# Sparse attention followed by an ELU layer pair: first loads in halves, four output tiles, and a new order of work

## The chip, the core and the metric

The kernel runs on one core of a Trainium2 chip. The core has five engines that run side by side, each with its own queue that it works off in order: TensorE (PE, matrix products into PSUM), VectorE (DVE), ScalarE (ACT, functions such as exp and ln, and copies), GpSimd (POOL, which here issues loads) and SyncE (SP, which here issues stores and DMA transposes). Transfers run on 16 DMA engines. The metric is the time of the device for one execution, in microseconds (us).

## The reference

Eight batches, eight heads, 576 positions, 64 features. Heads 0 to 3 see the last 32 positions (local), heads 4 to 7 every 32nd position back (strided). The result is laid out as 4608 tokens of 512 features and goes through two layers with an ELU between them.

```python
scores = scale * np.matmul(q, k.transpose(0, 1, 3, 2))
mask_local = (rel >= 0) & (rel < stride)
mask_strided = (rel >= 0) & (pos[None, :] % stride == pos[:, None] % stride)
scores = np.where(masks[None, :, :, :], scores, -1000000000.0)
attn = np.exp(scores - max); attn = attn / (sum(attn) + 1e-09)
x = np.matmul(attn, v)             # to (4608, 512)
h = x @ w_in                       # (512, 2048)
g = np.where(h > 0.0, h, np.exp(np.minimum(h, 0.0)) - 1.0)
out = g @ w_out                    # (2048, 512)
```

## The kernel before

**Tiles.** Tokens of a batch are held in eight interleaved sequences (`NS`), so that local and strided windows become small dense blocks. A *pair* is two heads of one kind of one batch: key `2s1` is batch 2, strided, pair 1; `l` is local. Each pair is worked in two halves, u = 0 and 1. q and k are transposed so that features lie on partitions (`qT`, `kT`); for batches 0 to 2 PE does this with an identity matrix and a copy out of PSUM, from batch 3 on a DMA transpose does it. The attention result goes to `xT`, features on partitions, all tokens. The layers run in nine *chunks* of 512 tokens: sixteen tiles m of the hidden layer, then four tiles kk of 128 output tokens.

**Order.** The order of all work is written out by hand in the string `ORDER` (lines 35 to 149), which a loop at the end (line 680) turns into calls. Since every engine works in the order in which its instructions were issued, this string is the queue of each engine. The letters: `w` warm-up matmuls on zeros; `F` masks; `K` cast of a staged head to bf16 (line 379; q on DVE, k on ACT); `T` transposes on PE (392, 395); `c`/`C` their copy out of PSUM on DVE/ACT (403 to 407); `S` scores (431); `e` exponential (438, ACT); `m` mask (445, 451, DVE); `O` product with v, with the row sums beside it (458 to 501); `n` logarithm of the sums (529, ACT); `r` exponential of its negative, which is the reciprocal (535, ACT); `x` multiplication into `xT` (560, DVE); `V`, `W` copies of v (564, 567, DVE); `D` loads (POOL); `X` DMA transposes (580, SP); `a`, `b`, `L` first layer (587: `a` the strided half of the features, `b` the local half, `L` both); `h` exponential (595, ACT); `i`/`j` clamp on DVE (604) or ACT (602); `g` the ELU's maximum (613, 615, DVE); `Z` a quarter of a second-layer tile (621), four of them a tile; `o`/`q` its copy to an output tile on ACT/DVE (627); `t` its store (639, SP); `Y`, `y` the last output tile in two column halves (647, 660 to 664). Digits after the key are PSUM banks: there are eight, and a bank is written again only when the copy, exponential or multiplication that reads it is done. `a.0.3.2` is the first layer of chunk 0, m = 3, in bank 2.

**Buffers.** Tile pools have a fixed number of buffers that go round: `p_ln` and `p_rc` two each (logarithm, reciprocal), `p_osb` two (output tiles), `p_he` four, `p_he1` three, `p_pm` five, `p_e` two. An instruction that writes a buffer waits until the last reader of its earlier content is done; for an output tile this reader is the store.

**Start.** The q and k of the first pair's kind are wanted first. Heads 0 and 1 of the strided q and k of batch 0 are loaded in f32 by SP into a staging area (the space of `g[0]`) and cast by `K`; heads 2 and 3 are loaded by POOL, whose DMAs cast on the way. Then POOL loads v, local q, local k and local v of batch 0, the four quarters of `w_in`, batch 1, and `w_out`. DVE meanwhile writes zeros and ones: with `fill_ones` (line 304) the columns of ones that stand beside v in both local v tiles and in the strided one, so that one matmul gives both the product and the row sums.

Of the kernel before, what the change touches and what calls it, by code (L numbers as in the profile page):

```python
# [15 lines left out]
S = 576  # L16
# [19 lines left out]
w.7.42 F.ms K.q.0 K.q.1 D.wi0.0 T.0s0.q.0 K.k.0 D.wi1.0 c.0s0.q K.k.1 T.0s1.q.7 D.wi2.0 T.0s0.k.0  # L36
c.0s1.q T.0s1.k.1 D.wi3.0 c.0s0.k c.0s1.k S.0s0.1.67 S.0s0.0.45 F.ml e.0s0.1 S.0s1.1.01 D.qs.1
S.0s1.0.23 e.0s1.1 m.0s0.1 e.0s0.0 O.0s0.1.67 m.0s1.1 e.0s1.0 O.0s1.1.01 m.0s0.0 D.ks.1 T.0l1.q.5
n.0s0.1 m.0s1.0 n.0s1.1 O.0s0.0.23 c.0l1.q r.0s0.1 T.0l0.q.4 r.0s1.1 x.0s0.1 n.0s0.0 D.vs.1
T.0l0.k.5 c.0l0.q r.0s0.0 O.0s1.0.67 x.0s1.1 C.0l0.k x.0s0.0 T.0l1.k.4 n.0s1.0 S.0l0.0.23 c.0l1.k  # L40
S.0l0.1.01 r.0s1.0 D.ql.1 e.0l0.0 V.0 S.0l1.1.45 e.0l0.1 m.0l0.0 S.0l1.0.23 x.0s1.0 e.0l1.1
O.0l0.0.01 m.0l0.1 m.0l1.1 n.0l0.0 O.0l0.1.45 e.0l1.0 O.0l1.1.67 r.0l0.0 m.0l1.0 n.0l1.1 D.kl.1
a.0.3.2 x.0l0.0 n.0l0.1 r.0l1.1 O.0l1.0.01 r.0l0.1 x.0l1.1 a.0.1.3 x.0l0.1 n.0l1.0 r.0l1.0 a.0.0.4
x.0l1.0 D.vl.1 b.0.3 a.0.5.0 h.0.3 b.0.5 i.0.3 g.0.3 a.0.6.1 D.wo0.0 h.0.5 a.0.11.5 i.0.5 b.0.11
g.0.5 a.0.10.2 h.0.11 b.0.6 i.0.11 a.0.4.0 h.0.6 g.0.11 b.0.4 D.wo1.0 a.0.13.7 i.0.6 h.0.4 b.0.13
g.0.6 a.0.15.5 h.0.13 i.0.4 D.wo2.0 b.0.15 g.0.4 j.0.13 a.0.2.6 b.0.2 h.0.15 g.0.13 b.0.0 h.0.2
D.wo3.0 i.0.15 a.0.7.0 h.0.0 i.0.2 b.0.7 g.0.15 b.0.10 h.0.7 a.0.12.7 D.qs.2 g.0.2 h.0.10 b.0.12
i.0.0 a.0.14.1 i.0.10 h.0.12 a.0.9.6 g.0.0 j.0.7 D.ks.2 b.0.9 g.0.10 T.1s0.k.4 h.0.9 T.1s0.q.5
i.0.12 a.0.8.2 c.1s0.k C.1s0.q b.0.1 D.ql.2 g.0.12 S.1s0.1.45 h.0.1 i.0.9 T.1l1.q.7 g.0.7 e.1s0.1
b.0.8 g.0.9 D.kl.2 T.1s1.k.0 h.0.8 T.1l0.q.4 m.1s0.1 j.0.1 T.1s1.q.6 c.1s1.k T.1l0.k.5 C.1l1.q g.0.1  # L50
b.0.14 C.1l0.k V.1 T.1l1.k.3 h.0.14 c.1s1.q D.vs.2 C.1l0.q c.1l1.k S.1s1.0.56 Z.0.3.0.7 e.1s1.0
i.0.14 i.0.8 S.1l1.0.56 m.1s1.0 S.1s1.1.34 e.1l1.0 Z.0.0.0.0 g.0.14 e.1s1.1 m.1l1.0 D.vl.2
O.1s1.0.56 g.0.8 O.1l1.0.34 n.1s1.0 Z.0.3.1.7 m.1s1.1 n.1l1.0 r.1s1.0 r.1l1.0 x.1s1.0 S.1l0.1.12
Z.0.0.1.0 x.1l1.0 e.1l0.1 m.1l0.1 S.1l1.1.12 O.1s1.1.34 e.1l1.1 O.1l0.1.56 Z.0.3.2.7 n.1s1.1 n.1l0.1
r.1s1.1 O.1s0.1.12 r.1l0.1 x.1s1.1 Z.0.0.2.0 n.1s0.1 m.1l1.1 r.1s0.1 x.1l0.1 O.1l1.1.34 x.1s0.1
Z.0.0.3.0 n.1l1.1 r.1l1.1 Z.0.3.3.7 x.1l1.1 o.0.0 Z.0.1.0.0 t.0.0 o.0.3 Z.0.1.1.0 t.0.3 Z.0.1.2.0
Z.0.1.3.0 Z.0.2.0.7 o.0.1 t.0.1 S.1l0.0.01 S.1s0.0.23 e.1l0.0 Z.0.2.1.7 W.2 e.1s0.0 Z.0.2.2.7
m.1l0.0 m.1s0.0 O.1l0.0.01 O.1s0.0.23 V.2 n.1l0.0 Z.0.2.3.7 n.1s0.0 r.1l0.0 r.1s0.0 T.2s1.k.4
x.1l0.0 o.0.2 T.2s0.k.5 c.2s1.k T.2s1.q.6 T.2s0.q.0 c.2s0.k C.2s1.q t.0.2 T.2l0.q.7 c.2s0.q D.qs.3
T.2l1.q.4 c.2l0.q S.2s0.0.01 S.2s1.0.56 c.2l1.q D.ks.3 e.2s0.0 T.2l1.k.7 x.1s0.0 T.2l0.k.4 e.2s1.0  # L60
D.vs.3 m.2s0.0 L.1.4.3 c.2l1.k C.2l0.k D.ql.3 O.2s0.0.12 m.2s1.0 h.1.4 L.1.2.0 n.2s0.0 i.1.4 X.qs.3
L.1.3.7 g.1.4 h.1.2 O.2s1.0.56 r.2s0.0 i.1.2 L.1.5.3 g.1.2 h.1.3 L.1.0.4 x.2s0.0 h.1.5 X.ks.3
n.2s1.0 L.1.6.0 i.1.3 i.1.5 h.1.0 g.1.3 L.1.7.1 h.1.6 i.1.0 L.1.11.7 r.2s1.0 i.1.6 D.kl.3 g.1.0
h.1.7 L.1.1.2 g.1.6 h.1.11 g.1.5 L.1.14.0 h.1.1 i.1.11 j.1.7 L.1.13.3 i.1.1 h.1.14 g.1.11 L.1.8.4
g.1.7 h.1.13 i.1.14 L.1.10.1 D.vl.3 g.1.1 h.1.8 X.ql.3 g.1.14 Z.1.0.0.2 h.1.10 i.1.13 j.1.8 i.1.10
Z.1.0.1.2 D.qs.4 g.1.13 L.1.15.0 g.1.8 g.1.10 S.2l0.0.34 h.1.15 L.1.9.7 x.2s1.0 D.ks.4 e.2l0.0
X.kl.3 i.1.15 S.2l1.0.56 h.1.9 S.2l1.1.34 m.2l0.0 L.1.12.1 e.2l1.0 g.1.15 e.2l1.1 m.2l1.0 O.2l0.0.56
Z.1.1.0.0 i.1.9 h.1.12 m.2l1.1 n.2l0.0 g.1.9 O.2l1.0.34 Z.1.1.1.0 i.1.12 n.2l1.0 g.1.12 Z.1.0.2.2
r.2l1.0 r.2l0.0 x.2l1.0 Z.1.0.3.2 x.2l0.0 O.2l1.1.34 o.1.0 Z.1.1.2.0 n.2l1.1 t.1.0 S.2s1.1.12
S.2s0.1.56 r.2l1.1 Z.1.1.3.0 e.2s1.1 x.2l1.1 X.qs.4 Z.1.2.0.7 e.2s0.1 m.2s1.1 o.1.1 S.3s0.0.34  # L70
m.2s0.1 O.2s1.1.56 e.3s0.0 O.2s0.1.01 Z.1.2.1.7 t.1.1 n.2s0.1 m.3s0.0 W.3 r.2s0.1 S.2l0.1.34 X.ks.4
Z.1.2.2.7 D.vs.4 e.2l0.1 x.2s0.1 Z.1.2.3.7 D.ql.4 n.2s1.1 m.2l0.1 O.2l0.1.01 r.2s1.1 q.1.2
O.3s0.0.34 Z.1.3.0.2 n.3s0.0 x.2s1.1 t.1.2 n.2l0.1 Z.1.3.1.2 r.3s0.0 S.3s0.1.56 r.2l0.1 D.kl.4
x.3s0.0 Z.1.3.2.2 e.3s0.1 x.2l0.1 S.3l1.0.34 S.3l0.1.56 e.3l1.0 m.3s0.1 L.2.7.7 e.3l0.1 m.3l1.0
L.2.2.3 h.2.7 m.3l0.1 i.2.7 L.2.1.6 h.2.2 D.vl.4 X.ql.4 g.2.7 L.2.13.5 i.2.2 h.2.1 g.2.2 L.2.3.7
h.2.13 i.2.1 D.qs.5 g.2.1 L.2.12.3 h.2.3 D.ks.5 i.2.13 O.3l1.0.01 i.2.3 h.2.12 L.2.9.6 g.2.13
n.3l1.0 g.2.3 L.2.0.5 X.kl.4 h.2.9 i.2.12 L.2.5.7 g.2.12 r.3l1.0 i.2.9 h.2.0 L.2.4.3 x.3l1.0 h.2.5
L.2.6.4 i.2.0 h.2.4 i.2.5 g.2.0 L.2.14.0 h.2.6 g.2.5 L.2.10.5 h.2.14 g.2.9 j.2.6 L.2.8.1 i.2.4
h.2.10 i.2.14 g.2.4 O.3s0.1.67 h.2.8 Z.1.3.3.2 g.2.6 n.3s0.1 L.2.11.3 i.2.8 r.3s0.1 i.2.10 g.2.8
L.2.15.4 h.2.11 g.2.10 o.1.3 Z.2.0.0.1 g.2.14 h.2.15 t.1.3 Z.2.0.1.1 x.3s0.1 j.2.11 j.2.15 g.2.11  # L80
O.3l0.1.67 Z.2.3.0.0 n.3l0.1 g.2.15 r.3l0.1 S.3s1.1.23 S.3s1.0.45 Z.2.0.2.1 X.qs.5 e.3s1.1 x.3l0.1
e.3s1.0 S.3l0.0.23 m.3s1.1 S.4s0.1.67 Z.2.0.3.1 m.3s1.0 e.3l0.0 e.4s0.1 X.ks.5 O.3s1.0.45 m.3l0.0
O.3s1.1.23 o.2.0 m.4s0.1 O.3l0.0.67 Z.2.3.1.0 W.4 n.3s1.0 n.3s1.1 Z.2.3.2.0 D.vs.5 t.2.0 r.3s1.0
D.ql.5 Z.2.3.3.0 r.3s1.1 x.3s1.0 n.3l0.0 Z.2.1.0.1 x.3s1.1 r.3l0.0 q.2.3 S.3l1.1.23 S.4l1.0.45
Z.2.1.1.1 e.3l1.1 x.3l0.0 t.2.3 e.4l1.0 O.4s0.1.23 D.kl.5 m.3l1.1 S.4s0.0.67 n.4s0.1 S.4s1.0.45
m.4l1.0 Z.2.1.2.1 e.4s1.0 Z.2.1.3.1 e.4s0.0 m.4s1.0 r.4s0.1 m.4s0.0 O.4s1.0.67 O.3l1.1.45 Z.2.2.0.0
n.4s1.0 x.4s0.1 n.3l1.1 D.vl.5 X.ql.5 q.2.1 O.4s0.0.23 Z.2.2.1.0 r.4s1.0 r.3l1.1 x.4s1.0 Z.2.2.2.0
n.4s0.0 x.3l1.1 D.qs.6 t.2.1 S.4s1.1.67 r.4s0.0 L.3.3.1 D.ks.6 e.4s1.1 x.4s0.0 L.3.1.4 h.3.3 m.4s1.1
X.kl.5 i.3.3 O.4s1.1.23 h.3.1 L.3.2.7 g.3.3 n.4s1.1 i.3.1 L.3.0.1 W.5 h.3.2 g.3.1 L.3.7.6 r.4s1.1
D.vs.6 i.3.2 h.3.0 L.3.4.4 g.3.2 h.3.7 i.3.0 L.3.6.7 i.3.7 h.3.4 g.3.0 j.3.4 L.3.8.5 g.3.7 h.3.6  # L90
D.ql.6 Z.3.0.0.1 g.3.4 h.3.8 i.3.6 L.3.5.4 i.3.8 g.3.6 L.3.9.6 g.3.8 h.3.5 X.qs.6 i.3.5 L.3.11.7
h.3.9 g.3.5 L.3.13.5 i.3.9 h.3.11 x.4s1.1 L.3.14.4 h.3.13 g.3.9 X.ks.6 j.3.11 S.4l0.0.23 i.3.13
Z.3.0.1.1 h.3.14 g.3.11 e.4l0.0 L.3.10.6 g.3.13 j.3.14 m.4l0.0 O.4l1.0.23 D.kl.6 g.3.14 h.3.10
L.3.15.7 n.4l1.0 i.3.10 O.4l0.0.45 g.3.10 Z.2.2.3.0 r.4l1.0 n.4l0.0 x.4l1.0 Z.3.0.2.1 r.4l0.0 q.2.2
S.4l1.1.23 L.3.12.6 e.4l1.1 x.4l0.0 t.2.2 h.3.15 S.5s0.0.23 m.4l1.1 S.5s0.1.45 h.3.12 Z.3.3.0.0
i.3.15 e.5s0.1 g.3.15 Z.3.3.1.0 e.5s0.0 i.3.12 m.5s0.1 O.4l1.1.23 m.5s0.0 O.5s0.1.45 n.4l1.1 g.3.12
Z.3.3.2.0 r.4l1.1 Z.3.0.3.1 n.5s0.1 x.4l1.1 O.5s0.0.67 Z.3.3.3.0 o.3.0 n.5s0.0 t.3.0 S.4l0.1.12
q.3.3 r.5s0.1 Z.3.2.0.3 X.ql.6 r.5s0.0 x.5s0.1 Z.3.1.0.0 e.4l0.1 x.5s0.0 S.5s1.0.45 S.5s1.1.12
m.4l0.1 S.5l1.0.67 e.5s1.0 Z.3.1.1.0 X.kl.6 e.5l1.0 m.5s1.0 O.4l0.1.45 e.5s1.1 m.5l1.0 O.5s1.0.67
Z.3.2.1.3 D.vl.6 n.4l0.1 m.5s1.1 t.3.3 O.5l1.0.12 r.4l0.1 Z.3.2.2.3 n.5l1.0 x.4l0.1 Z.3.2.3.3 D.qs.7  # L100
n.5s1.0 r.5l1.0 D.ks.7 L.4.0.4 q.3.2 r.5s1.0 L.4.3.5 x.5l1.0 t.3.2 h.4.0 x.5s1.0 L.4.6.1 h.4.3 i.4.0
L.4.14.6 i.4.3 h.4.6 g.4.0 X.qs.7 L.4.11.7 g.4.3 h.4.14 i.4.6 L.4.4.2 h.4.11 i.4.14 g.4.6 j.4.11
L.4.10.5 g.4.14 X.ks.7 h.4.4 L.4.5.1 g.4.11 h.4.10 i.4.4 L.4.8.7 i.4.10 h.4.5 g.4.4 L.4.1.6 g.4.10
h.4.8 j.4.5 i.4.8 L.4.2.2 h.4.1 g.4.8 L.4.13.5 g.4.5 h.4.2 i.4.1 L.4.9.7 h.4.13 i.4.2 g.4.1 L.4.15.1
h.4.9 g.4.2 j.4.13 L.4.12.6 i.4.9 h.4.15 g.4.9 L.4.7.2 h.4.12 i.4.15 g.4.13 O.5s1.1.34 h.4.7
Z.4.3.0.7 g.4.15 n.5s1.1 i.4.7 Z.3.1.2.0 i.4.12 r.5s1.1 g.4.7 Z.3.1.3.0 W.6 g.4.12 S.6l1.0.12 D.vs.7
o.3.1 Z.4.3.1.7 x.5s1.1 e.6l1.0 D.ql.7 t.3.1 S.5l0.0.56 S.6s1.0.01 m.6l1.0 S.5l1.1.34 e.5l0.0
# [605 lines left out]
```

## Time and profile before

| | us |
|---|---|
| three timed runs | 315.68, 316.15, 316.51 (median 316.15) |
| the profiled execution | 316.63 |
| its span, first to last instruction | 314.9 |
| mean granted TensorE clock, share of full | 0.978 |

The page divides the span into 40 slices of 7.9 us. DMA engines are over nine tenths busy in almost all slices to about 190 us and nearly idle after it. Some rows by stage (busy us of each engine, granted clock as a share of full speed):

| stage, us | PE | DVE | ACT | PEclk |
|---|---|---|---|---|
| 5 to 10 | 3.02 | 4.29 | 2.20 | 0.79 |
| 10 to 21 | 10.16 | 8.58 | 9.70 | 0.50 |
| 21 to 22 | 1.00 | 0.00 | 0.00 | 0.75 |
| 22 to 38 | 15.48 | 15.12 | 13.11 | 1.00 |
| 40 to 60 | 18.31 | 8.70 | 11.78 | 1.00 |
| 80 to 100 | 18.25 | 13.57 | 16.47 | 1.00 |
| 140 to 160 | 19.03 | 15.16 | 17.30 | 1.00 |
| 160 to 180 | 20.00 | 18.57 | 15.99 | 1.00 |

In the second part of a profile line such as `L627 ACT COPY osb<-ps ... x26 | 15.2, 584 | 27.0` stand the busy time of the group in us, the mean of one instruction in ns, and the time for which the engine stood idle just before them. Matmuls overlap, so a matmul's own duration (379 ns for 512 columns) is longer than the time after which the next one starts. In the chain of waits each line is what the next one had to wait for. A line in the list of waits reads: who, for whom, us in total, how many times, the longest.

### The profile page before, as it was taken

The numbers are of one execution on the slowest core, as the hardware profiler recorded it, in microseconds if no ns is written. First come the engines' busy times: TensorE is split into PE (matmuls) and PEld (weight loads), VectorE is DVE, ScalarE is ACT, GpSimd is POOL, SyncE is SP. The second block draws the span as 40 slices with busy tenths as digits, with TensorE's granted clock in tenths as the row PEclk, the third lists the DMA queues.
The fourth block names the chain that finished last, engine by engine and source line by source line (L and its number), as shares of the span: only waits on it lengthen the run. The fifth ranks groups of instructions, "written<-read, shape, count | busy, mean of one in ns | idle before, by whom it ended". The sixth has DMA issues, their size and how long they took to land.

```text
span 314.9 us, 6470 instructions
## 1 busy us (share of the span) xinstructions
PE 302.4 (96%) x2426; PEld 153.3 (49%) x2426; DVE 226.3 (72%) x448; ACT 231.9 (74%) x404; POOL 71.8 (23%) x99
## 2 busy tenths in 40 slices
PE   6899997999979999999899999999999999999995
PEld 6744553644534455444454454455445544444444
DVE  7859961799758987899579966995993359971500
ACT  3867882797977899978788799898865877862411
POOL 8533310363074009407140342000000000000000
PEclk9569999999999999999999999999999999999999
DMA  8999999499999999999998199002102220002123
GB/s 165 192 207 203 197 206 212 88 159 127 138 199 166 164 144 165 147 144 140 168 154 166 13 179 176 11 0 69 34 0 69 69 67 1 0 2 67 33 78 92
DMA packets 96009, 36.30 MB, mean 115 GB/s; under 512 B 77642, under 2 KB 91178, under 8 KB 95978
## 3 DMA queue, kind: packets, MB, share of 16 engines
q0 software_dynamic: 64016, 19.40, 60.3%
q1 hardware_dynamic: 31878, 16.42, 28.9%
q8 instruction: 19, 0.31, 0.4%
q14 instruction: 12, 0.10, 0.1%
q10 hardware_dynamic: 84, 0.07, 0.1%
HBM read 39.41 MB, written 9.44 MB: 155 GB/s over the span
## 4 chain that ended last, share of the span: by engine, by line
PE 78%; DVE 9%; DMA 7%; ACT 3%; issue 2%; SPq 0%; DVEq 0%; ACTq 0%
PE ps L587 36%; PE ps L621 32%; DMA out_dram<-osb 7%; PE ps L431 3%; DVE g L615 2%; PE ps L501 2%; PE ps L494 2%; DVE he L604 1%; DVE xT L560 1%; PE ps L395 1%; PE ps L458 1%; PE ps L474 1%; ACT ln L529 1%; PE ps L392 1%; ACT osb L627 1%
## 5 line engine op out<-in xcount | busy, mean ns | idle before, releaser
L621 PE MATMUL ps<-w_out_sb,g 128*128 128x512 bf16 x560 | 131.6, 379 | 0.9 <-DVE osb L627 0.9
L587 PE MATMUL ps<-xT,w_in_sb 128*128 128x512 bf16 x576 | 130.9, 382 | 0.1
L595 ACT ACTIVATE he<-ps 128x512 f32<-128x512 f32 x144 | 84.6, 595 | 30.1 <-PE ps L587 27.9
L587 PEld LDWEIGHTS <-w_in_sb 128*128 128x128 bf16 x576 | 55.2, 98 | 65.8 <-issue 2.1
L621 PEld LDWEIGHTS <-g 128*128 128x128 bf16 x560 | 50.8, 98 | 56.3 <-issue 1.5
L615 DVE TENSOR_TENSOR g<-he,ps 128x512 bf16<-128x512 bf16 x114 | 75.5, 682 | 1.6
L560 DVE TENSOR_TENSOR xT<-ps,rc 64x576 bf16<-64x576 f32 (+1 forms) x64 | 42.8, 679 | 28.1 <-ACT rc L535 27.6
L604 DVE TENSOR_SCALAR he<-he 128x512 bf16<-128x512 f32 x114 | 47.1, 429 | 16.8 <-ACT he L595 16.0
L438 ACT ACTIVATE e<-ps 128x576 bf16<-128x576 f32 (+1 forms) x64 | 39.4, 647 | 7.7 <-PE ps L431 6.8
L535 ACT ACTIVATE rc<-ln 64x576 f32<-64x576 f32 (+1 forms) x64 | 38.7, 621 | 2.9 <-DVE xT L560 1.6
L529 ACT ACTIVATE ln<-ps 64x576 f32<-64x576 f32 (+1 forms) x64 | 36.4, 585 | 4.4 <-PE ps L474 1.7
L627 ACT COPY osb<-ps 128x512 f32<-128x512 f32 x26 | 15.2, 584 | 27.0 <-PE ps L621 20.6
L613 DVE SCALAR_TENSOR_TENSOR g<-he,ps 128x512 bf16<-128x512 bf16 x30 | 20.3, 681 | 0.6 <-ACT he L602 0.6
L451 DVE TENSOR_TENSOR pm<-e,mask_l 128x576 bf16<-128x576 bf16 x32 | 14.4, 454 | 6.8 <-ACT e L438 6.2
L602 ACT ACTIVATE he<-he 128x512 bf16<-128x512 f32 x30 | 18.7, 628 | 0.6
L239 POOL DMA_DIRECT2D ql<-in_q_dram x20 | 16.3, 824 | 8.6 <-DMA qTl<-ql 8.6
L445 DVE TENSOR_TENSOR pm<-e,mask_s 72x576 bf16<-72x576 bf16 x32 | 14.3, 452 | 3.6 <-ACT e L438 2.8
L246 POOL DMA_DIRECT2D kl<-in_k_dram x20 | 15.2, 780 | 5.8 <-DMA kTl<-kl 2.2
L233 POOL DMA_DIRECT2D vs<-in_v_dram x7 | 4.8, 687 | 44.0 <-DVE vsp L567 42.4
L256 POOL DMA_DIRECT2D vl<-in_v_dram x8 | 9.5, 1183 | 18.8 <-PE ps L501 13.4
L627 DVE COPY osb<-ps 128x512 f32<-128x512 f32 x9 | 6.2, 688 | 7.1 <-DMA out_dram<-osb 5.2
L431 PEld LDWEIGHTS <-kTl 64*128 64x128 bf16 x192 | 5.4, 98 | 11.3 <-issue 9.5
(83 smaller groups left out, 170.4 us busy)
## 6 DMA issues: line engine op xcount, KB each, us to landing
out_dram<-osb SPq DMA_DIRECT2D x31, 144.0 KB
vl<-in_v_dram POOLq DMA_DIRECT2D x8, 288.0 KB, 9.4
w_in_sb<-in_moe_w_in_dram POOLq DMA_DIRECT2D x4, 512.0 KB, 12.7
w_out_sb<-in_moe_w_out_dram POOLq DMA_DIRECT2D x4, 512.0 KB, 15.1
vs<-in_v_dram POOLq DMA_DIRECT2D x6, 320.0 KB, 7.6
qs<-in_q_dram POOLq DMA_DIRECT2D x5, 320.0 KB, 11.0
ks<-in_k_dram POOLq DMA_DIRECT2D x5, 320.0 KB, 11.0
ql<-in_q_dram POOLq DMA_DIRECT2D x20, 72.0 KB, 7.6
```

The lines of the kernel that those rows point to most:

```text
L438: nc.scalar.activation(e[0:R], tiles.pop(("S", key, u))[0:R], ACT.Exp, scale=scale)
L529: nc.scalar.activation(t, s_ps, ACT.Ln)
L535: nc.scalar.activation(t, tiles.pop(("ln", key, u)), ACT.Exp, scale=-1.0)
L560: nc.vector.tensor_mul(dst, o_ps, rc)
L587: nc.tensor.matmul(tiles["h", ch, m], lhsT=w_in_sb[:, c, m * 128:(m + 1) * 128], rhs=xT[:, c, ch * CHUNK:(ch + 1) * CHUNK], start=(c == 2) ...
L595: nc.scalar.activation(e, tiles["h", i[0], i[1]], ACT.Exp)
L602: nc.scalar.activation(e1, e, ACT.Relu, bias=1.0, scale=-1.0)
L604: eng.tensor_scalar(e1, e, scalar1=1.0, scalar2=1.0, op0=ALU.min, op1=ALU.subtract)
L613: nc.vector.scalar_tensor_tensor(dst, e1, -1.0, h, op0=ALU.mult, op1=ALU.max)
L615: nc.vector.tensor_tensor(dst, e1, h, op=ALU.max)
L621: nc.tensor.matmul(ops, lhsT=g[ch % 2][:, m, kk * 128:(kk + 1) * 128], rhs=w_out_sb[:, m, :], start=(m == 0), stop=(m == MC - 1), skip_gro ...
L627: eng(o_sb, tiles.pop(("o", int(ch), int(kk))))
```

## The change

1. The stage loads go in halves of each run: a run of a token row is 512 values (eight tokens of a partition), and `load_stage` now loads columns 0 to 255 and 256 to 511 of q and k as four DMAs, in the order q, k, q, k. `K` (q, DVE) and `k` (k, ACT) cast one half of both heads; the first pair's transposes, copies and first scores are done by halves; its first scores use 72 columns of kT as weights, where all others use 128.
2. Four output tiles in place of two. The reciprocal is written over the logarithm: `p_rc` is gone, `p_ln` has three tiles.
3. `ones` is filled first; the columns of ones of the strided v tile and of the second local v tile are written by ACT copies from it, where DVE memsets wrote them. The local q and k of batch 0 are loaded in two DMAs each, where each was one.
4. The string `ORDER` is new throughout. It has 34 warm-up matmuls (42 before), 106 clamps on DVE and 38 on ACT (114 and 30), 22 output copies on ACT and 13 on DVE (26 and 9), and 22 and 4 copies of transposes on DVE and ACT (17 and 7). The matmuls of the layers, the scores and the products with v are the same in number.

```diff
-w.7.42 F.ms K.q.0 K.q.1 D.wi0.0 T.0s0.q.0 K.k.0 D.wi1.0 c.0s0.q K.k.1 T.0s1.q.7 D.wi2.0 T.0s0.k.0
-c.0s1.q T.0s1.k.1 D.wi3.0 c.0s0.k c.0s1.k S.0s0.1.67 S.0s0.0.45 F.ml e.0s0.1 S.0s1.1.01 D.qs.1
...
+w.7.34 F.ms K.q.0 k.k.0 T.0s0.q.0.0 K.q.1 C.0s0.q.0 T.0s0.k.1.0 k.k.1 c.0s0.k.0 T.0s0.q.0.1
+T.0s1.q.1 c.0s0.q.1 D.wi0.0 S.0s0.0.23 c.0s1.q T.0s1.k.0 e.0s0.0 D.wi1.0 T.0s0.k.1.1 c.0s1.k
+c.0s0.k.1 S.0s1.0.67 m.0s0.0 S.0s1.1.45 D.wi2.0 e.0s1.0 S.0s0.1.01 F.ml O.0s0.0.23 e.0s1.1 m.0s1.0
...
-    p_ln = ctx.enter_context(tc.tile_pool(name="p_ln", bufs=2))
-    p_rc = ctx.enter_context(tc.tile_pool(name="p_rc", bufs=2))
+    p_ln = ctx.enter_context(tc.tile_pool(name="p_ln", bufs=3))
...
-    p_osb = ctx.enter_context(tc.tile_pool(name="p_osb", bufs=2))
+    p_osb = ctx.enter_context(tc.tile_pool(name="p_osb", bufs=4))
...
+    HF = NS * D // 2
+
+    def load_stage(i, u, x):
+
         rows, in_ = runs(x, 0, HG, 2)
         nc.sync.dma_start(
-            out=stage[0:rows, i * 2 * NS * D:(i + 1) * 2 * NS * D].rearrange(
-                "p (h f) -> p h f", h=2), in_=in_)
-
-    load_stage(0, q)
-    load_stage(1, k)
+            out=stage[0:rows, (2 * i + u) * 2 * HF:(2 * i + u + 1) * 2 * HF].rearrange(
+                "p (h f) -> p h f", h=2),
+            in_=bass.AP(in_.tensor, in_.offset + u * HF, [[NS * D, rows], [S * D, 2], [1, HF]]))
+
+    for u in range(2):
+        load_stage(0, u, q)
+        load_stage(1, u, k)
...
+    def fill_ones(t, n, eng=None):
         w = t.bitcast(F32)
...
+            if eng is None:
+                nc.vector.memset(dst, two)
+            else:
+                src = ones.bitcast(F32)[0:dst.shape[0]].unsqueeze(1)
+                eng(dst, src.to_broadcast([dst.shape[0], dst.shape[1], D // 2]))
+
+    nc.vector.memset(ones, 1.0)
+    fill_ones(vl_t[0], HG * LB)
+    fill_ones(vs_p, HG * NS, nc.scalar.copy)
+    fill_ones(vl_t[1], HG * LB, nc.scalar.copy)
     for t in vl_t:
-        fill_ones(t, HG * LB)
         nc.vector.memset(blocks(t, HG * LB)[0:PRE, 0, :], 0.0)
-    for nm in ("vs", "ql", "kl", "vl"):
-        load(nm, 0)
-    fill_ones(vs_p, HG * NS)
+    load("vs", 0)
+    for y in range(2):
+        for nm in ("ql", "kl"):
+            load_runs(nm, 0, 2 * y, 2)
+    load("vl", 0)
...
+    def cast(eng, nm, u):
+        i, u = "qk".index(nm), int(u)
+        eng(raw[nm + "s"][0:RS].rearrange("p (h f) -> p h f", h=HG)[:, 0:2, u * HF:(u + 1) * HF],
+            stage[0:RS, (2 * i + u) * 2 * HF:(2 * i + u + 1) * 2 * HF].rearrange(
+                "p (h f) -> p h f", h=2))
...
+                if u is not None and sp // 2 != int(u):
+                    continue
...
+    def copy_T(eng, key, nm, u=None):
         P = Pair(key)
-        t = tiles.pop(("T", key, nm))
+        t = tiles.pop(("T", key, nm, u))
+        if u is not None:
+            dst, c0 = (P.qT, P.q0) if nm == "q" else (P.kT, P.k0)
+            dst, t = (z.rearrange("c (x w) -> c x w", x=2)[:, :, int(u) * W // 2:(int(u) + 1) * W // 2]
+                      for z in (dst[:, c0:c0 + S], t))
+            eng(dst, t)
+            return
...
+        M = RS if (key, u) == ("0s0", 0) else 128
...
-        t = tiles["rc", key, u] = p_rc.tile([128, 2, W], F32, tag="rc", name="rc")[rows, 0:n]
-        nc.scalar.activation(t, tiles.pop(("ln", key, u)), ACT.Exp, scale=-1.0)
+        t = tiles["rc", key, u] = tiles.pop(("ln", key, u))
+        nc.scalar.activation(t, t, ACT.Exp, scale=-1.0)
```

## The prediction

> **What bounds the kernel now.** I read the head of the page first, to see which engine fills the span and where it does not run at full rate.
>
> ```profile
> PE 302.4 (96%) x2426; PEld 153.3 (49%) x2426; DVE 226.3 (72%) x448; ACT 231.9 (74%) x404; POOL 71.8 (23%) x99
> PEclk9569999999999999999999999999999999999999
> ```
>
> TensorE (PE) is busy 96% of the span, the others at most 74%: a microsecond counts only where PE stands idle, or where its granted clock is low (slices 2 and 3, 8 to 24 us). The change leaves PE's work as it is, so everything it can win lies in those places. So I read next who PE waited for, over the whole span.
>
> ```profile
> PE ps L431 <- DVE xT L560: 1.7, 1, 1.7
> PE ps L431 <- ACT osb L627: 1.7, 1, 1.7
> PE ps L392 <- DVE qs L379: 1.2, 2, 0.8
> PE ps L373 <- DVE zero L295: 1.1, 1, 1.1
> PE ps L621 <- DVE osb L627: 0.9, 1, 0.9
> ```
>
> The three large waits behind the start are each one event. The chain of waits between 80 and 96 us shows what is behind the one named xT (columns: start, length, what):
>
> ```profile
> 82.77 0.59 ACT osb L627
> ...
> 83.99 8.05 DMA out_dram<-osb
> ...
> 92.32 0.10 DVE osb L627
> ...
> 93.04 0.77 DVE xT L560
> ...
> 93.85 0.31 PE ps L431 x8
> ```
>
> A PSUM bank of output is copied to an output tile (L627) only when that tile's earlier store has landed. There are two tiles. The store issued at 83.4 us landed at 92.0, the VectorE (DVE) copy stood in front of its queue until then, the multiplication into xT stood behind it, and PE behind that. The wait on ACT's copy ends the same way (store 49.04 to 54.10, copy 54.20, PE 54.84), and so does the third (store 147.58 to 154.10, copy 154.29, PE 155.03). Last the start, from the timeline (start, length, engine, line):
>
> ```profile
> 5.11 1.48 DVE L379 CAST qs<-g 72x512 bf16<-72x512 f32 x2
> 5.62 1.14 ACT L379 CAST ks<-g 72x512 bf16<-72x512 f32 x2 [3.53 <-DMA g<-in_k_dram]
> 8.47 1.14 PE L431 MATMUL ps<-qTs,kTs 64*128 64x72 bf16 x32
> 8.94 2.41 ACT L438 ACTIVATE e<-ps 72x576 bf16<-72x576 f32 x4 [2.18 <-PE ps L431]
> ```
>
> DVE casts as soon as its fills end (5.19), ACT when k lands. The first exponential runs at 8.94; from there to the last multiplication of batch 0 (20.45 to 20.91) ACT is the busiest engine (9.70 of 11 us between 10 and 21).
>
> **Four output tiles.** PE's loss at the three places, by its own rows: a dense 512-column matmul takes 0.216 us (108 in 23.31 us of the chain). The last run before each wait started at 49.74 with 15, 90.21 with 8 and 153.08 with 4 matmuls, so PE had no work from 52.98, 91.94 and 153.94, and went on at 54.84, 93.85 and 155.03: 1.86 + 1.91 + 1.09 = 4.86 us. (The waits view gives 1.7 + 1.7 + 0.9 = 4.3, as it models the ends later.) With two tiles a copy comes in the old order as little as 3.45 us of PE work behind the store two copies earlier (o.0.1 behind t.0.0). Counting PE work by rows along the new order, each copy lies at least 11.2 us behind the store four copies earlier (o.7.1, o.8.1), and over 26 us in most cases. Stores landed in 5.06 to 8.05 us. So the wait goes: **-4.86**, with -4.3 and, were a new wait to take half, -2.4 as ends. What is next there: DVE copies batch 2's v (L567), and behind that copy in its queue stand the first transposed tiles of batch 2. That copy waited 4.9 us for its load and ran at 53.1. By PE work PE gets to batch 2's first transposes at about 52, and needs the tiles some 4 us later: free by about 2 us.
>
> SP's own queue: the new order issues the same stores and 20 DMA transposes (up to 5.5 us each on SP) between them; a store stuck behind one now costs nothing up to the margin above. The first scores of batches 3 to 7 lie at least 16 us of PE work behind the transposes that they read (15 in the old order).
>
> **Halves of the first pair.** Two stage DMAs of 320 KB become four of half the size on SP (two issues more of 0.4 us), the q halves cast on DVE, the k halves on ACT. Where a first half lands no row shows; k's end at 5.62 after an issue at 0.81 to 1.67 bounds it above, and half the bytes by 3.9 us would be even progress. DVE loses 0.91 + 0.70 + 0.09 + 0.09 us of fills to ACT, but its small fill of the second vl tile now waits for ACT's fill of it. ACT copies cost 0.266 us for 128 and 0.585 for 512 elements, so 0.83 ns an element and 0.16 us: 1024, 32, 768 and 32 elements take 1.01 + 0.19 + 0.80 + 0.19 = 2.19, from the end of the table load (2.09) to 4.28. Behind it DVE has 0.09, the kT fills (0.35) and the mask (0.65): the first cast starts at 5.37, 0.2 later than now. From there: cast 0.78 to 6.15, four transposes 0.30, ACT's copy of 288 elements 0.40; meanwhile the second cast to 6.9, DVE's copy of the k half to 7.2, pair 0s1's transposes to 7.45, the first half's scores 0.30, the exponential at 7.9. That is 1.0 us before 8.94. But the next one needs 0s1's k, which DVE copies only at about 8.5, so the four exponentials end near 10.85 against 11.35 now. From there ACT does the same 25-odd instructions as before. I take **-0.5**; ends -1.0 (the whole lead kept) and +0.3 (the later DVE start, nothing else).
>
> The weights limit what more could be had: w_in's quarters, issued from 7.1 us, took 10.0 to 15.4 us to land, 17.1 to 24.8. The bytes ahead of them are unchanged; POOL has two issues more (0.64 each), while its earlier loads are still landing. The first batch's q of the next attention landed near 26.3 and is wanted at about 27 in the new order.
>
> **Log and reciprocal in one tile.** p_ln has three tiles, held from the log to the multiplication (0.645 + 0.68 + 0.754 = 2.1 us), in place of two and two. ACT needs 1.32 us for a log and its reciprocal, so three hold 3.96. Nothing, ends -1.6 (the one wait of L535 for L560 in the waits view) and +1.5 (two waits of one 0.754 multiplication).
>
> **The order.** Eight warm-up matmuls less (0.1 each, before any data). Eight clamps go from DVE to ACT (-3.4, +5.0), four output copies the other way (+2.75, -2.3), four bank copies of transposes net to DVE. Neither engine is full over the span (72%, 74%), so nothing while PE's queue covers it. Where DVE binds is 22 to 38 us (15.12 busy of 16). Adding rows along each engine's order, a DVE result that PE needs there comes up to 2.45 us behind PE in the old order, 1.88 in the new one from the same kind of count; counted from the first layer's start alone 2.02 and 2.75. I take 0, ends -0.6 and +0.7.
>
> **Sum.** The profiled execution took 316.63 (span 314.9 and 1.73 around it): 316.63 - 4.86 - 0.5 = 311.27. It lies 0.48 above the median 316.15; I take off half of that: **311.0**.
>
> **Rivals.** (1) *The stall moves.* The copies are no longer late, but the loads of the next batches, the transposes on SP and the stores now meet on DMA engines that are already 90% busy to 190 us, and PE meets one of them instead. For: the stores took 5 to 8 us in that stretch against 1.6 at the end. Against: PE has no wait on a load in the whole profile. Half of the 4.86 comes back: 313.4. The Trainium skill (DMA: Bandwidth & Descriptors, "Issuing engines are not separate DMA queues") says that whichever queue starts them, transfers interleave on the same 16 engines; the landing times above agree.
>
> (2) *Slower: the clock stays at half through chunk 0.* The rows by stage show 1.00 to 7 us, 0.50 from 8 to 21 and 1.00 from 22. PE goes idle now from 5.2 and gets its clock back only after it is dense from 18 us. The new order ends its warm-up at about 4.4, starts real work at 6.15, and puts transposes of batch 1, which wait for loads, between the first-layer matmuls. Each us at 0.50 costs 0.5 us of PE work; 16 us more of it than now, as long as the stage from 22 to 38, cost 8: 316.63 - 5.4 + 8 = 319.2. It decides from 10.7 us more of half clock on (0.5 x 10.7 = 5.4). Against: the new order has the same density after 18 us by PE work. The skill (TensorE: Matmul & The Clock Gate, Part 1) has the clock go back up after about 3.4 us of sustained work and fall after an idle window of that length, which speaks against so long a hold; the rise at 21.5, 3.5 us after 18.0, agrees.
>
> (3) *Nothing to measure.* The new order gives the 5 us back in many small waits of the pools and banks, as the old one lost 0.2 to 0.5 in a dozen places: 316.2.
>
> (4) *More.* Lead of 1 us kept, chunk 0 0.6 better, the small waits fewer (1.5): 308.5.
>
> **Chances.** Forecast 0.62, (1) 0.13, (4) 0.05: faster 0.80. (3) 0.05, within 0.3%, about 0.95 us, which is what a measurement here can tell from no change. (2) 0.15. The forecast's own range is 309.5 to 312.8 (sum of its ends: -1.3 to +1.8). The range to hold 8 in 10 takes in (1) and reaches to no change: 308.8 to 316.3.
>
> **What would show it.** Right: no wait of L627's successor on a store, PE without gaps near 53, 92 and 154 us, the first exponential near 7.9 and the last log of batch 0 about 0.5 us earlier than 19.9, full clock again near 22. Wrong: PE waits on DVE's copy of v or on a transposed tile after 50 us (1); PEclk with more than three slices of 5 (2); the first cast after 6 us, so that ACT's fills cost more than the halves win.

## The result and the profile after

The changed kernel took a median of 312.78 us in one set of runs and 312.92 in a second, against 316.33 and 316.67 for the kernel before beside it. The ratios are 0.9887 (95% interval 0.9839 to 0.9935) and 0.9906 (0.9872 to 0.9939): 3.0 to 3.8 us faster, where 311.0, 5.2 faster, was forecast. Ratios leave disturbed executions out, while the medians given are of all executions; two of the profiles read below (by_head's and warm_3's) are of such executions, and no kernel time is read from them.

The head of the page and the list of PE's waits for the profiled execution (311.83 us, span 310.1). The columns of the waits are the waiting instruction, what it waited for, microseconds in total, times, longest:

```profile
PE 297.5 (96%) x2379; PEld 152.9 (49%) x2418; DVE 225.2 (73%) x445; ACT 232.0 (75%) x409; POOL 72.1 (23%) x101
PEclk9999999999999999999999999999999999999999
```
```profile
PE ps L406 <- DVE qs L390: 2.2, 2, 1.6
PE ps L642 <- issue: 1.4, 9, 0.2
PE ps L385 <- DVE zero L299: 1.1, 1, 1.1
...
```

The three waits that ended on an output tile are gone: no line names osb, or the multiplication into xT (now L581). The largest entry left is on the first pair's q, and it grew from 1.2 to 2.2 us. Two things in this profile must not be taken at their word. It has 2379 matmul records beside 2418 weight loads, so PE's busy time is short by the missing ones. And it shows a full clock throughout, while its matmuls of 8 to 20 us have the lengths of half clock (the first one of the first layer, at 19.66, takes 0.61 us, a later one 0.38). The second profile of the same kernel, after_again, has all records and the usual clock.

The busy time of PE around the three old waits (columns: stretch in us, its length, busy us and instructions, granted clock, DMA share, GB/s), in the kernel before, the changed kernel (after_again), and two experiments told below:

```profile
48.00:60.00 12.00, 10.31 (x120) 1.00 0.97 153
86.00:98.00 12.00, 10.25 (x101) 1.00 1.54 176
148.00:160.00 12.00, 11.03 (x109) 1.00 1.65 188
```
```profile
48.00:60.00 12.00, 12.00 (x178) 1.00 1.22 189
86.00:98.00 12.00, 12.00 (x82) 1.00 1.47 150
148.00:160.00 12.00, 12.00 (x103) 1.00 1.23 167
```
```profile
48.00:60.00 12.00, 12.00 (x182) 1.00 1.01 173
86.00:98.00 12.00, 11.91 (x93) 1.00 1.51 174
148.00:160.00 12.00, 12.00 (x103) 1.00 0.98 135
```
```profile
48.00:60.00 12.00, 11.70 (x175) 1.00 1.18 180
86.00:98.00 12.00, 12.00 (x91) 1.00 1.47 175
148.00:160.00 12.00, 12.00 (x104) 1.00 0.79 131
```

From the first fence to the second PE gains 1.69 + 1.75 + 0.97 = 4.41 us of work in the three stretches. The third is the kernel before with four tiles, the fourth the changed kernel with two. All three changed versions fill the holes.

The start is where the forecast's mechanism goes wrong. The timeline of the changed kernel (start, length, engine, line; in brackets what ended the engine's idle time, and how long that was):

```profile
4.02 0.61 ACT L390 CAST ks<-g 72x512 bf16<-72x512 f32 x1
4.92 0.53 DVE L390 CAST qs<-g 72x512 bf16<-72x512 f32 x1
6.79 0.92 DVE L390 CAST qs<-g 72x512 bf16<-72x512 f32 x1 [1.34 <-DMA g<-in_q_dram]
8.02 0.62 ACT L390 CAST ks<-g 72x512 bf16<-72x512 f32 x1 [1.65 <-DMA g<-in_k_dram]
9.10 0.65 ACT L459 ACTIVATE e<-ps 72x576 bf16<-72x576 f32 x1 [0.46 <-PE ps L452]
```

The first halves come early (k cast at 4.02, against 5.62 for whole k before). The second halves come late: both engines wait for them, to 6.79 and 8.02, where the prediction had them landed by 5.6. So the first exponential runs at 9.10 (8.77 in the second profile) and not at 7.9; before it ran at 8.94. The last logarithm of batch 0 ends at 19.97 in the second profile, against 19.95 before: the front has won nothing.

### The profile page after: what moved, and what is told of

Same layout as the page of the kernel before. It is cut to its first block, busy times and chain, and to the rows that moved or that the text cites. A ratio compares the mean times of both kernels' runs of the same rounds, so it can differ in the third digit from the quotient of the medians.

```text
span 310.1 us, 6379 instructions
## 1 busy us (share of the span) xinstructions
PE 297.5 (96%) x2379; PEld 152.9 (49%) x2418; DVE 225.2 (73%) x445; ACT 232.0 (75%) x409; POOL 72.1 (23%) x101
## 4 chain that ended last, share of the span: by engine, by line
PE 83%; DMA 7%; ACT 4%; DVE 3%; issue 2%; SPq 0%; ACTq 0%; DVEq 0%
PE ps L608 39%; PE ps L642 33%; DMA vl<-in_v_dram 5%; PE ps L452 3%; PE ps L515 2%; PE ps L522 2%; ACT e L459 2%; DMA g<-in_q_dram 2%; PE ps L668 1%; ACT ln L550 1%; PE ps L406 1%; PE ps L409 1%; ACT ln L556 1%; DVE xT L581 1%; DVE kTl L427 1%
## 5 line engine op out<-in xcount | busy, mean ns | idle before, releaser
L642 PE MATMUL ps<-w_out_sb,g 128*128 128x512 bf16 x539 | 128.4, 379 | 2.1 <-issue 1.4
L608 PE MATMUL ps<-xT,w_in_sb 128*128 128x512 bf16 x558 | 128.2, 380 | 1.6 <-issue 0.6
L636 DVE TENSOR_TENSOR g<-he,ps 128x512 bf16<-128x512 bf16 x106 | 70.2, 684 | 1.5
L581 DVE TENSOR_TENSOR xT<-ps,ln 64x576 bf16<-64x576 f32 (+1 forms) x64 | 42.3, 677 | 13.3 <-ACT ln L556 11.4
L625 DVE TENSOR_SCALAR he<-he 128x512 bf16<-128x512 f32 x106 | 44.1, 430 | 10.2 <-ACT he L616 9.7
L459 ACT ACTIVATE e<-ps 72x576 bf16<-72x576 f32 (+1 forms) x64 | 39.6, 645 | 8.6 <-PE ps L452 7.1
L556 ACT ACTIVATE ln<-ln 64x576 f32<-64x576 f32 (+1 forms) x64 | 38.6, 621 | 1.2
L634 DVE SCALAR_TENSOR_TENSOR g<-he,ps 128x512 bf16<-128x512 bf16 x38 | 25.8, 683 | 0.7 <-ACT he L623 0.3
L623 ACT ACTIVATE he<-he 128x512 bf16<-128x512 f32 x38 | 23.6, 627 | 1.1 <-DVE g L636 0.3
L648 DVE COPY osb<-ps 128x512 f32<-128x512 f32 x13 | 9.0, 691 | 6.6 <-PE ps L642 6.3
```

The source lines that it names most:

```text
L459: nc.scalar.activation(e[0:R], tiles.pop(("S", key, u))[0:R], ACT.Exp, scale=scale)
L556: nc.scalar.activation(t, t, ACT.Exp, scale=-1.0)
L581: nc.vector.tensor_mul(dst, o_ps, rc)
L608: nc.tensor.matmul(tiles["h", ch, m], lhsT=w_in_sb[:, c, m * 128:(m + 1) * 128], rhs=xT[:, c, ch * CHUNK:(ch + 1) * CHUNK], start=(c == 2) ...
L623: nc.scalar.activation(e1, e, ACT.Relu, bias=1.0, scale=-1.0)
L625: eng.tensor_scalar(e1, e, scalar1=1.0, scalar2=1.0, op0=ALU.min, op1=ALU.subtract)
```

## The experiments

**Four tiles or the rest of the change?** The first question was whether the four tiles or the rest, the new order above all, removes the stalls. In the changed kernel the output pool gets its two tiles back; in the kernel before it gets four.

```
-    p_osb = ctx.enter_context(tc.tile_pool(name="p_osb", bufs=4))
+    p_osb = ctx.enter_context(tc.tile_pool(name="p_osb", bufs=2))
```

> The changed kernel with two output tiles in place of four, all else the same. Theory: the gain is the removed wait for output tiles; in the new order a copy then stands as little as 4.0 us of PE work behind the store two copies earlier, so PE waits on output copies come back at places where stores take 5 to 8 us, and about 4 to 6 us of the gain is lost: 316 to 318. Rival: the new order spreads the copies so that the tiles no longer matter, and it stays within 1 us of the changed kernel (312 to 314).

Measured: 313.68 us (313.03 over the nine executions that the ratio compares), ratio 0.9906 (0.9869 to 0.9943). The stalls stay away, as the last of the four fences above shows. Counting PE's work by its rows along the new order, a copy comes at least 4.6 us behind the store two copies earlier (o.6.1 behind t.5.1; the expectation has 4.0), against 3.45 in the old one, both without the last tile, and the pinch is elsewhere. Two copies on ACT still waited for a store, 0.99 us to 55.07 and 0.82 us to 123.56, but PE waited for no output tile.

```
-    p_osb = ctx.enter_context(tc.tile_pool(name="p_osb", bufs=2))
+    p_osb = ctx.enter_context(tc.tile_pool(name="p_osb", bufs=4))
```

> The kernel before with four output tiles, nothing else. Theory: the three gaps of PE near 53, 92 and 154 us go (1.86 + 1.91 + 1.09 = 4.86 us), no other wait takes their place: 311 to 312.5, as fast as the changed kernel, and the rest of the change is worth nothing. Rival: after the first gap PE runs into loads of the next batch or into other waits; it gains 2 to 3 us: 313.5 to 314.5.

Measured: 313.31 us against 316.27, ratio 0.9909 (0.9877 to 0.9941). One number in the code gives 3.0 us, most of the whole change. The four tiles take the stalls away without the rest of the change, and the rest does so without them; together they cannot do it twice. That it is the order within the rest is argued from the distances above, not tried by itself.

The sum's largest term was 4.86. Profile against profile the four tiles give 316.63 - 312.32 = 4.31, median against median 2.96. Here is a reason that I can argue but not show: the compared executions of the kernel before spread from 313.8 to 318.3 in this set, those with four tiles from 312.3 to 314.3. The stores' landing times (5.06 to 8.05 us) and thus the stalls would differ from one execution to the next. The two profiled executions explain the difference only as numbers: the one before was 0.36 above its median, and the one with four tiles, at 312.32, was the fastest of its nine and 0.99 below. Why the median gains 1.9 less than the three stalls were long stays open.

**Why do the second halves come late?** Two ideas first: a half's rows are 1 KB in place of 2 KB, or four DMAs go worse than two. Whole loads keep one DMA for q and one for k, but cast, transpose and copy in halves:

```
...
-    for u in range(2):
-        load_stage(0, u, q)
-        load_stage(1, u, k)
+    load_stage(0, q)
+    load_stage(1, k)
...
```

> The changed kernel with the staged q and k loaded by one DMA each, whole runs of 2 KB; casts, transposes and scores stay in halves. Theory: the second halves came late (the cast of the second q half began at 6.79 us and that of the second k half at 8.02, where all of k was there at 5.62 before) because of the split loads; with whole loads q is there by 5.1 and k by 5.6, the first exponential moves from 9.10 to about 7.4, and the end by 0.3 to 1.0 us: 311.8 to 312.5. Rival: the DMA queues as a whole are late here and the split is not the cause; the first exponential stays near 9 and the time at 312.8.

Measured: 311.82 us, ratio 0.9876 (0.9836 to 0.9916). q is cast from 4.93, both halves without a wait, k from 5.65, and the first exponential runs at 8.21. Four DMAs with rows of 2 KB, one for each head:

```
...
-        rows, in_ = runs(x, 0, HG, 2)
+        rows, in_ = runs(x, 0, HG + h, 1)
...
```

> The changed kernel with the staged loads in four DMAs still, but each one head with whole runs of 2 KB; every cast of a half then waits for both heads of q or of k. Theory A: the 1 KB rows make the split loads slow; with 2 KB rows the last k lands at 5.6 to 6.0. Theory B: four DMAs of the queue make them slow, whatever their rows; the last k lands near 8.0 again. The time is within 1 us of the changed kernel either way (312 to 313.5).

Measured: 314.0 us, ratio 0.994 (0.9897 to 0.9983), above the expected 313.5. The second pieces are late again: DVE waits to 6.51 for q, ACT's first cast of k waits to 7.71. So it is not the 1 KB rows. What remained was a queue that serves its DMAs one by one, or POOL's loads, the first of which is issued at 1.36 us, ahead of the third (1.73) and the fourth (2.22) staged DMA. Two runs to tell these apart, with the changed kernel itself beside them:

> The changed kernel unaltered, as the measure for the three beside it: 312.8 us as before, ratio to the kernel before 0.989. Second q half cast at 6.8 us, second k half at 8.0 us, first exponential at 9.1 us. If the front's times in this second profile differ by over 0.3 us, single profiles cannot order the front's variants.

Measured: 312.92 us, ratio 0.9906 (0.9872 to 0.9939); second halves cast at 7.35 and 7.72, first exponential at 8.77. The front's times move by up to 0.6 us between two profiles of one kernel, more than the 0.3 set for ordering variants by single profiles. Only differences well above that are used here.

```
-        nc.sync.dma_start(
+        (nc.sync, nc.scalar)[i].dma_start(
```

> The changed kernel with the two staged DMAs of k issued by ACT's queue, so that SP's and ACT's queues hold two each; same rows, same bytes. Theory (a queue serves its DMAs one behind the other, and the third and fourth pay for that): the second q half lands near 5.5 us instead of 6.8 and its cast starts there, the second k half before 6.5; ACT's table load and fills come about 0.9 us later, so the first exponential near 8.3; time 312.0. Rival (the loads that POOL issues from 1.4 us on take the DMA engines at 3 to 4 us): landings stay at 6.8 and 8.0, time 312.8 or, for ACT's two issues, up to 313.3.

Measured: 312.02 us, ratio 0.9883 (0.9832 to 0.9933). The first exponential runs at 8.03. The test is not clean: ACT's two issues pushed its fills back, DVE's small fill waited for them to 5.00, and q was cast only from 5.92, now without waiting for data. The last k half was cast at 7.03, behind a copy in ACT's own queue (6.73) and not behind data.

```
-    load_runs("qs", 0, 2, 2)
-    load_runs("ks", 0, 2, 2)
...
-    fill_ones(vl_t[1], HG * LB, nc.scalar.copy)
+    fill_ones(vl_t[1], HG * LB, nc.gpsimd.tensor_copy)
...
+    load_runs("qs", 0, 2, 2)
+    load_runs("ks", 0, 2, 2)
+    load("vs", 0)
...
```

> The changed kernel with POOL's loads for batch 0 issued behind its mask work and behind the fill of the second v tile, which POOL takes over from ACT: POOL's first DMA comes over 1.5 us later. Theory (the third and fourth staged DMA are late by their own queue): second halves still land at 6.5 to 6.8 and 7.7 to 8.0. Rival (they are late because POOL's loads take the DMA engines): they land by 5.0 and 5.6. Both: the second pair's tiles come later by what POOL is late, so the time is 313.5 to 315.

Measured: 313.98 us, ratio 0.993 (0.9897 to 0.9964). The timeline of this kernel, POOL's first load now at 3.18 us:

```profile
3.47 0.41 DVE L390 CAST qs<-g 72x512 bf16<-72x512 f32 x1
4.15 0.62 ACT L390 CAST ks<-g 72x512 bf16<-72x512 f32 x1 [0.89 <-DMA g<-in_k_dram]
4.63 0.42 DVE L390 CAST qs<-g 72x512 bf16<-72x512 f32 x1 [0.74 <-DMA g<-in_q_dram]
5.44 0.62 ACT L390 CAST ks<-g 72x512 bf16<-72x512 f32 x1
7.54 0.65 ACT L459 ACTIVATE e<-ps 72x576 bf16<-72x576 f32 x1 [1.49 <-PE ps L452]
```

Same queue, same four DMAs, same rows, and the second halves are cast 2.2 and 2.6 us earlier than in the changed kernel's first profile (2.7 and 2.3 than in its second), far more than the 0.6 between these two. The queue's own service is refuted; they were late because POOL's loads had been issued ahead of them. The rates at which data moved between 0 and 8 us show it too (40 equal slices of 0.2 us; first the changed kernel, then this one):

```profile
GB/s 0 0 0 0 0 0 0 0 0 102 174 338 282 266 338 200 26 67 41 92 118 97 128 215 236 241 261 246 266 251 246 230 190 159 184 184 184 189 210 195
```
```profile
GB/s 0 0 0 0 0 0 0 0 0 113 266 307 190 251 333 328 348 184 174 205 205 246 113 31 97 77 77 148 174 200 164 174 200 200 123 82 61 61 72 118
```

In the first the rate falls to 26 to 128 GB/s from 3.2 to 4.6 us, when half of the staged bytes have landed and POOL's first loads come in; in the second it holds until 4.4, through all four, and the dip follows when POOL's loads start. The first exponential then runs at 7.54, near the predicted 7.9, although PE waited 0.9 us for POOL's q on the way; the time is no better, for PE pays for POOL's lateness:

```profile
PE ps L488 <- DMA vs<-in_v_dram: 1.6, 1, 1.6
...
PE ps L406 <- DMA qs<-in_q_dram: 0.9, 1, 0.9
PE ps L409 <- DMA kl<-in_k_dram: 0.7, 1, 0.7
```

Every load of batch 0 is wanted soon; what one gains by going first, another loses.

**The halves undone.** Loads, casts, transposes and copies of the first pair whole, everything else as changed; the core is the order's opening rows:

```
-w.7.34 F.ms K.q.0 k.k.0 T.0s0.q.0.0 K.q.1 C.0s0.q.0 T.0s0.k.1.0 k.k.1 c.0s0.k.0 T.0s0.q.0.1
-T.0s1.q.1 c.0s0.q.1 D.wi0.0 S.0s0.0.23 c.0s1.q T.0s1.k.0 e.0s0.0 D.wi1.0 T.0s0.k.1.1 c.0s1.k
-c.0s0.k.1 S.0s1.0.67
+w.7.34 F.ms K.q.0 k.k.0 K.q.1 T.0s0.q.0 k.k.1 c.0s0.q T.0s0.k.1 T.0s1.q.0 c.0s0.k D.wi0.0
+S.0s0.0.23 c.0s1.q T.0s1.k.1 e.0s0.0 D.wi1.0 c.0s1.k
+S.0s1.0.67
```

> The changed kernel with the first pair's q and k loaded, cast, transposed and copied whole, as in the kernel before (cast by head); the four tiles, the reciprocals, the fills on ScalarE and the order from the second exponential on stay. This is the halves' step alone, undone. The prediction's step (halves are worth 0.5 us) gives 313.3. Theory now (the halves' second DMAs are late, so as built they win nothing against whole loads with whole casts): first exponential near 9 us as in the changed kernel, time 312.5 to 313.1. Rival (halves are worth over 1 us even so): 313.9 or more.

Measured: 312.27 us, ratio 0.9893 (0.9858 to 0.9929). Its front:

```profile
4.92 1.01 DVE L388 CAST qs<-g 72x512 bf16<-72x512 f32 x2
5.47 1.14 ACT L388 CAST ks<-g 72x512 bf16<-72x512 f32 x2 [1.36 <-DMA g<-in_k_dram]
7.96 0.65 ACT L456 ACTIVATE e<-ps 72x576 bf16<-72x576 f32 x1 [1.35 <-PE ps L449]
```

Without halves the first exponential runs at 7.96, earlier than with them, where near 9 was expected. In time the halves cannot be told from nothing: the median is 0.5 to 0.65 us below the changed kernel's, the ratio lies between its two, and the intervals cover one another.

**Fills, and the two queues again.** Whole loads with all fills back on DVE:

```
-    fill_ones(vs_p, HG * NS, nc.scalar.copy)
-    fill_ones(vl_t[1], HG * LB, nc.scalar.copy)
+    fill_ones(vs_p, HG * NS)
+    fill_ones(vl_t[1], HG * LB)
```

> Whole staged loads (q and k one DMA each, casts and transposes still in halves) and all fills back on VectorE. Theory (the fills moved to ScalarE are worth little, because q lands near 4.9 us anyway): the casts of q start at 4.9 to 5.4 us, the first exponential at 8.2 to 8.7, time 311.8 to 312.3, within 0.2% of whole loads with the fills on ScalarE (311.8). Rival (VectorE's fills were what held the front): casts of q after 5.9 us, time 312.8 or more.

Measured: 312.61 us, ratio 0.9879 (0.9833 to 0.9925), over 310.5 to 313.6. q is cast from 5.07, 0.14 later than with ACT's fills, the first exponential runs at 8.33. DVE's fills did not hold the front. The median is above the expected range, but the ratio is that of whole loads.

Whole loads with k issued on ACT's queue, at the same 0.8 us as q:

> Whole staged loads as in whole loads, q on SP's queue and k on ACT's, both issued at 0.8 us; casts and transposes in halves. Theory (what counts is that the staged pieces are issued ahead of POOL's first load at 1.4 us): k lands 0.3 to 0.5 us earlier than the 5.6 of whole loads, the first exponential at 7.8 to 8.1 instead of 8.2, time 311.4 to 311.9. Rival (the sum of bytes decides, not the issue): k still at 5.6, and ACT's fills 0.45 us later hold VectorE's cast of q, so that the first exponential is at 8.4 or later and the time 312.2 or more.

Measured: 311.8 us, ratio 0.9877 (0.9835 to 0.9919). The time was in the range, the mechanism was not: k was cast from 6.11 and q from 5.85 after a wait for data, both later than with one queue (5.65 and 4.93). Only q's difference (0.9) is above the 0.6 between two profiles of one kernel. It fits two loads that share the way when they are started together, while with one behind the other the first is there for DVE as the second lands; no other run tests this.

Whole loads and whole loads with k on ACT's queue have the lowest medians of all, about 1.0 us below the changed kernel's. The two other kernels with whole loads, the one with all fills on DVE (312.61) and the one without halves (312.27), lie 0.2 to 0.65 below it, and the intervals of all four overlap with its own. That whole loads make a better version than the changed kernel is likely, not shown.

**The clock.** What is batch 0's half clock worth, and can it be avoided? To whole loads, matmuls on zeros were added, three or eight ahead of each of 19 groups of scores, transposes and sums of batch 0, and ten more in the opening row (here the version with eight):

```
...
-c.0s0.k.1 S.0s1.0.67 m.0s0.0 S.0s1.1.45 ...
+c.0s0.k.1 w.7.8 S.0s1.0.67 m.0s0.0 w.7.8 S.0s1.1.45 ...
```

> Whole loads with three matmuls on zeros ahead of each group of scores, transposes and sums of batch 0 from the second block of scores on (57 more), and ten more in the opening row. They change no output. The clock was 0.50 from about 8.5 to 22 us in the profiles that record it; 57 matmuls of 128 columns are 3.0 us at full clock (0.053 each, from the opening row after 3.3 us) and 6.1 at half. Theory A (batch 0's small tiles do not count as enough work, the added ones do): the clock holds or rises several us earlier than 22, the first-layer matmuls from 19 us on run at 0.215 us each at once, time 310.5 to 311.5. Theory B (the clock's return is set by something else, or three are too few): half clock to 22 us or later, PE is late by up to 6 us less its idle time, time 314 to 317.

Measured: the twelve executions fall into nine of 319.0 to 321.0 us with a mean clock of 0.961 to 0.968, and three of 312.8 to 314.0 with 0.999 to 1.000. The ratio, 0.9895 (0.9841 to 0.9948), rests on these three. The profile is of the first kind; PE by stretches (length, busy, clock as above):

```profile
8.00:20.00 12.00, 11.45 (x179) 0.53 1.43 197
20.00:28.00 8.00, 7.59 (x83) 0.50 1.24 206
28.00:32.00 4.00, 3.78 (x15) 0.84 1.45 195
```

> The same with eight at each place (152 more: 8.1 us at full clock, 16.3 at half). Theory A: the clock stays at 1.00 from 4 us on, batch 0's real work takes half the time, and the first layer starts at 20 to 21 us at full clock, time 311 to 313. Theory B: half clock, the first layer starts near 30 us, time 320 or more.

Measured: 318.05 us, ratio 1.0059 (1.0024 to 1.0094). The first two of these stretches, and a row of groups for the sums of a local window (busy, mean ns), first of this kernel and then of the one with three:

```profile
8.00:20.00 12.00, 11.16 (x238) 1.00 1.43 196
20.00:28.00 8.00, 7.31 (x111) 1.00 1.24 206
```
```profile
L495 PE MATMUL ps<-pm,ones 128*64 128x288 bf16 x8 | 1.3, 310 | 0.0
```
```profile
L495 PE MATMUL ps<-pm,ones 128*64 128x288 bf16 x8 | 1.8, 448 | 0.0
```

With eight the clock holds, and here the record can be believed: the same matmul takes 310 ns, not 448. It is not worth it: 318.05 is 6.2 us above whole loads (5.8 by the two ratios), and both expected times, 311 to 313 and 320 or more, were missed. The first layer starts at 26.41 us, 7.51 later than in whole loads (18.90). What the added matmuls cost is read from the timeline, from the start of a group of eight to the start of what follows:

```profile
8.01 0.61 PE L385 MATMUL ps<-zero 128*128 128x128 bf16 x8
8.55 0.30 PE L452 MATMUL ps<-qTs,kTs 64*128 64x72 bf16 x8
```

The 19 groups held PE's queue for 10.4 us in this way, 0.55 each, more than the 8.1 that 152 matmuls at 0.053 us would give. So the rest of batch 0 became 10.4 - 7.5 = 2.9 us shorter on a full clock. (At half clock the same reckoning finds no gain, as it should: with three, the groups held the queue for 8.2 us, and the first layer started 8.7 later, at 27.64.) The kernel as a whole is another 1.3 us less late than its first layer, since that layer does not begin at half clock. The half clock of this stage thus costs about 10.4 - 6.2 = 4 us. This is an estimate from single profiles, and rather a high one, since a part of the added matmuls fills time in which PE would have waited for ACT and DVE; and more than twice that has to be paid to avoid it.

## Why the prediction was right, and where not

*Four output tiles, -4.86.* The place and the cause were right: three waits on landed stores, gone. The size was not, and this is the largest error of the sum: 4.86 was read from one execution, where the runs give 2.96 by medians for the tiles alone. Of the ends given, -4.3 is what the profiles show and the -2.4 is near the medians. The prediction took the stall of one execution at its full length as the loss of all; what the others lost was not recorded. It also put all of the gain down to the tiles, where the rest of the change without them does as much: its count of distances compared two tiles in the old order with four in the new and left out two in the new.

*Halves, -0.5.* This step failed, in its assumption that the pieces progress evenly, half by 3.9 and the rest by 5.6 us. The rest came at 6.8 to 8.0, behind POOL's loads. Undone, the halves are worth nothing that can be told (312.27 without them). The estimate of ACT's fills was good: 4.28 predicted, 4.11 measured. The first q cast came at 4.92, earlier than the predicted 5.37. The chain behind the first cast was costed at 2.5 us (5.37 to 7.9); where it did not wait for data, in k_on_act, it took 2.1 (5.92 to 8.03).

*Log and reciprocal in one tile, 0.* ACT's 1.6 us wait for a multiplication is gone from the waits, and PE never waited for it. The part was not tried by itself.

*The order, 0.* Not separable here beyond the stalls: the changed kernel less its halves is at 312.27, the kernel before with four tiles at 313.31, with intervals that overlap.

*The sum.* 311.0 was 1.8 below the first median. The stalls account for 1.9 of that (4.86 against 2.96), the halves for 0.5; the rest of the change, fills and order together, brought back about the 0.5 to 1.0 us that separates it from four tiles alone. These parts come from medians of several sets and hold to about half a microsecond. That the time came out near the forecast is thus in part luck, as the last part was put at nothing: the first median lies just inside the forecast's own range (312.8 at its upper end), the second, 312.92, just outside. (The lower end of that range should read 309.7: 311.0 - 1.3.)

*The rivals.* (1) The stall did not move: in the two profiles of the changed kernel the waits of PE on a load or a transposed tile after 50 us are of 0.2 us each, one in either (on a copy of qTs in the first, on kTl at 117 us in the second). By the letter of the sign that was given for this rival they count, but their size is nothing. The time that this rival gave, 313.4, was as near as the forecast's, for another reason. On the other hand its rule, cited from the Trainium skill (DMA: Bandwidth & Descriptors, "Issuing engines are not separate DMA queues"), applies at the front: transfers of SP's queue and of POOL's share the engines, and pool_later measures it at 2.2 to 2.6 us. (2) The clock did not stay at half: two slices of 5 in after_again's page, against a 5 and a 6 before. The windows put its return at 21.5 us in the kernel before and at 22.4 in after_again, as predicted ("near 22"). But its price, 0.5 us for each us of half clock, holds only where PE is the bound; in batch 0 it is about 2.9 us over the 10 us of half clock, by the estimate from the run with eight added matmuls.

## What to carry to other kernels

A stall that is read in one profile is one execution's stall, and removing it gave less here than its length: where it hangs on how long a transfer takes, look at the spread of the times before putting it in a sum in full. When a buffer is waited for, ask how far apart its uses lie in the order, as well as how many buffers there are; here either change cured it, and not twice. A load split into pieces has its later pieces issued later, behind whatever other queues have put in by then: split only if nothing else is issued in between, or order the issues of all queues together.

## What the runs showed of the hardware

Batch 0's stream of small tiles did not raise the granted clock, although PE's record is nearly full. In after_again it was at 0.50 from 8.8 us on, with PE busy 11.14 of the 12 us from 8 to 20, and returned at 22.4, after the 128x512 matmuls of the first layer had begun at 19.26. So the sustained work by which rival (2) has the clock go back up is not busy time in this record. Matmuls of 128x128 on zeros, eight to a group, held the clock at 1.00; with three to a group it was at 0.50 to beyond 28 us in the one execution profiled. How long after the first layer's start the clock returns varies: 3.5 us in the kernel before (18.0 to 21.5), 3.2 in after_again, 2.8 in old_front (18.5 to 21.3), 0.6 in k_on_act (18.4 to 19.0). The Trainium skill (TensorE: Matmul & The Clock Gate, Part 1) says that activity is judged in a window of about 3.4 us that runs freely and is not set by the kernel; a spread from near 0 to 3.5 us would fit that, but no run here shows the window itself. It may also be a part of the spread between executions: by the price of half clock where PE is the bound, 2.9 us more of it would be an estimated 1.4 us of time. The four figures are of four kernels, so this is not shown.

A profile's clock record can be empty of the very changes: the changed kernel's first profile shows 1.00 throughout and matmul lengths of half clock. The lengths decide.
